# Token-major keys without TensorE: VectorE block transposes and ScalarE copies from unit 8 on, with 112-wide value tiles

## The chip, the cores and the metric

The kernel runs on one core of one Trainium2 chip. The metric is device microseconds of one execution. TensorE (PE) does matmuls and loads weights (PEld), VectorE (DVE) and ScalarE (ACT) do elementwise work, GpSimd (POOL) only sets constants up, and SyncE (SP) issues nearly all DMA transfers; the finished output is sent by ScalarE.

## The reference

The program is a gated linear attention with a complex decay, followed by a gated feed-forward layer without a nonlinearity. There are 4 batches, 8 heads, 768 tokens and a head width of 48; the feed-forward layer goes from 384 (8 x 48) to 1,536 and back for all 3,072 tokens.

```python
mag = np.sqrt(a_re * a_re + a_im * a_im)
scale = np.minimum(mag, 0.999) / (mag + 1e-06)
a_re_n, a_im_n = (a_re * scale, a_im * scale)
for t in range(S):
    new_re = ar * S_re - ai * S_im
    new_im = ar * S_im + ai * S_re
    S_re, S_im = (new_re + k[t] outer v[t], new_im)
    y[:, :, t] = np.einsum('bhd,bhde->bhe', q[:, :, t], S_re)
x = y with the heads side by side, one row per token
return (x @ w_a) * (x @ w_b) @ w_out
```

All arrays are 32-bit floats.

## The kernel before

**Units.** The 3,072 tokens are cut into 12 units of 256: unit u holds chunk u % 6 (128 tokens) of two batches. For each unit there are three stages. Unit 5 and unit 11 are the last chunks of their batch pairs; they hand no state on.

**Preparation, `prep(u)`** (L200), mostly VectorE with some ScalarE. It scales the decays of the unit (`scale`, L167, a chain of ScalarE functions and VectorE products that uses the tile `a_t` of another unit as scratch), forms their running complex products (L227, L233 over 8 tokens, then L262 and L268 over the 16 blocks, then L289 and L294), takes reciprocals (L297 to L320), and multiplies keys and queries by them in the tile `qk` (L324, and L309 in `times_p`). Keys and queries have the feature in the partition and the token in the free dimension: `qk` is [128, 3, 2, 514], three groups of 128 features, real and imaginary part, 256 query tokens and 256 key tokens. The scaling of the next unit's decays is interleaved with the products of this unit, from the fifth step of the loop at L224 on. `prep` ends with the load of the decays of unit u + 2 (L333), into the buffer that `a_t` of this unit leaves (two buffers).

**Stacking, `stack(u)`** (L338): ten SyncE DMA issues copy `qk` into `stk`, where each head has its 96 rows (48 real, 48 imaginary) in partitions 0 to 95.

**Attention, `attn(u)`** (L365), for each batch i of the two and each half of the heads: score matmuls (L379) and their causal masking by VectorE (L382); TensorE transposes of the keys against an identity (L390) and ScalarE copies of them from PSUM into tiles `kt`, token-major, two buffers (L394); output matmuls of values with masked scores and of the old state with the queries (L422), whose sum ScalarE and VectorE split in two parts `xh` and `xl` (L424, L430); and the state update, matmuls of `kt` with the values (L445), added to the state tiles `us` (L452, L456). Units 5 and 11 leave out transposes and states.

Values arrive as tiles of 512 columns, 128 for each pair of heads: head one in columns 0 to 47, head two in 80 to 127, zeros between. The state tiles are laid out alike.

**Feed-forward**: `gemm1` (L483) computes for each of 12 slices f of the hidden layer both products, 18 matmuls into a PSUM tile `ab` (three buffers); ScalarE copies one half out (`h_t`, L497, two buffers), VectorE multiplies it by the other half (L498), and ScalarE and VectorE split the product into `hh` and `hl` (L499, L500). `gemm2` (L503) multiplies these with the output weights two slices later (`LAG`). ScalarE copies the finished output into `o_sb` (L646, three buffers, which also serve the weight conversion at the start) and sends it.

**Order.** The loop over w (L650) runs the feed-forward of unit w and, from slice 6 on (5 for w = 0), the attention of unit w + 1, piece by piece between the slices. After slice 10 (11 in the first three turns) the rest of the preparation of unit w + 2 is written, then its stacking, then the load of keys and queries and the start of the preparation of unit w + 3. A planner then sets the order of each engine's queue from priorities and estimated durations; score masking, output matmuls and the copies of the feed-forward have raised priority (`ATTN_FIRST`, `MOE_FIRST`). Within a queue, instructions run in that order, and a waiting one holds those behind it.

The load of the values of unit w + 1 stands at the start of the turn:

```python
t = vpool.tile([128, 512], F32, name="v_t")
sync.dma_start(out=t, in_=v_d[u, i])
```

Of the kernel before, what the change touches and what calls it, by code (L numbers as in the profile page):

```python
# [19 lines left out]
C = 128  # L20
# [15 lines left out]
A2_MAX = 2.0 ** 60  # L36
ST = 8
# [8 lines left out]
OWN_FROM = 2  # L46
O_BUFS = 3
# [20 lines left out]
def tile_kernel(ctx: ExitStack, tc: tile.TileContext, a_d, qk_d, v_d, w_d, qn_d, kn_d, vn_d, an_d, out_d):  # L68
# [40 lines left out]
    us = [const.tile([128, 512], F32, name=f"u{i}") for i in range(2)]  # L109
# [90 lines left out]
    def prep(u):  # L200
# [23 lines left out]
        for i in range(1, SUB):  # L224
            pr = small.tile([128, 2, 2, NB], F32, name="pr", bufs=1)
            for o, n in parts:
                vec.tensor_tensor(  # L227
                    out=pr[:, :, :, o:o + n],
                    in0=view(zz, W + at_(i) + 2 * o, [[W, 2], [-W, 2], [2, n]]),
                    in1=tok(slice(1, 3), i - 1, o, n).unsqueeze(1).broadcast_to([128, 2, 2, n]),  # L230
                    op=ALU.mult)
            for o, n in parts:
                vec.tensor_tensor(out=tok(slice(1, 3), i, o, n), in0=pr[:, :, 0, o:o + n],  # L233
                                  in1=pr[:, :, 1, o:o + n], op=ALU.add)
            yield 440 + (next(sg, 0) if i > 3 else 0)
        for _ in sg:
            pass
# [11 lines left out]
        vec.tensor_scalar(out=tt[:, 0], in0=tt[:, 2], scalar1=-1.0, scalar2=None, op0=ALU.mult)  # L249
        if c == 0:  # L250
            b_t = small.tile([128, 3, G, NSB], F32, name="b_t")
            vec.memset(b_t[:, 1, :, 0], 1.0)
            vec.memset(b_t[:, 2, :, 0], 0.0)
        else:
            b_t = bnext.pop(u)
# [27 lines left out]
        yield 1600  # L283

# [44 lines left out]
        for k in range(2):  # L329
            times_p(k, 0 if u else 1, 2)  # L330
            yield 1670
# [20 lines left out]
    def load_v(u):  # L352
        for i in range(2):
            t = vpool.tile([128, 512], F32, name="v_t")
            sync.dma_start(out=t, in_=v_d[u, i])
            v_tiles[u, i] = t
# [3 lines left out]
    for g in range(H // 2):  # L360
        for q, pieces in ((3 * g, [(2 * g, 0)]), (3 * g + 1, [(2 * g + 1, 96)]),
                          (3 * g + 2, [(2 * g, 32), (2 * g + 1, 64)])):
            quads[q % 4].append((q // 4, [(h, g * 128 + off) for h, off in pieces]))

    def attn(u, xh, xl):  # L365
# [3 lines left out]
        ams, kts, xps = {}, {}, {}  # L369
# [16 lines left out]
        def transposes(i, hg):  # L386
            qs, ks = cols(i)
            tp = ps_m.tile([128, 512], F32, name="pm")
            for h4 in range(4):
                pe.transpose(out=tp[:, h4 * KS:(h4 + 1) * KS], in_=stk[0:KS, hg * 4 + h4, ks],  # L390
                             identity=ident[0:KS, 0:KS])
            kt = kvp.tile([128, 4, KS], F32, name="kt", bufs=2)
            with tc.high_priority(offset=ATTN_FIRST):
                act.copy(out=kt.rearrange("p h k -> p (h k)"), in_=tp[:, 0:4 * KS])  # L394
            kts[i, hg] = kt
# [41 lines left out]
        def state(i, hg):  # L437
# [4 lines left out]
            for h4 in range(4):  # L442
                h = hg * 4 + h4
                o = (h // 2) * 128 + (h % 2) * (80 if own else 32)
                pe.matmul(out=kp[0:KS, h4 * n:(h4 + 1) * n], lhsT=kts[i, hg][:, h4, :],  # L445
                          rhs=v_t[:, o:o + n], start=True, stop=True)
            uv = view(ut[0:KS], hg * 256, [[128, 2], [80, 2], [1, 48]])
# [19 lines left out]
        for fn, i, g in order:  # L467
            if not (last and fn in (transposes, state)):
# [3 lines left out]
    def pieces(u):  # L472
        return 8 if u % NCH + 1 == NCH else 16
# [9 lines left out]
    def gemm1(f, xh, xl, ps_ab=ps_ab, moe=moe):  # L483
# [9 lines left out]
        h_t = moe.tile([128, TOK], F32, name="h_t")  # L493
# [154 lines left out]

    pgen = None
    for w in range(NU):  # L650
# [18 lines left out]
        for f in range(NF):  # L669
# [8 lines left out]
            pend.append((w, f, *gemm1(f, *x_cur), os_))  # L678
# [89 lines left out]
```

## Time and profile before

| what | value |
|---|---|
| median of 3 runs | 691.08 us (691.05 to 691.49) |
| the profiled execution's own time | 690.18 us |
| its span in the profile | 688.5 us |
| granted TensorE clock, mean | 0.972 |
| TensorE busy | 644.5 us (94%) |
| VectorE busy | 550.1 us (80%) |
| ScalarE busy | 310.1 us (45%) |
| transposes on TensorE (L390) | 160 recorded, 251 ns each as recorded |
| copies of them on ScalarE (L394) | 40 recorded, 482 ns each |

Matmuls overlap in the pipeline, so their recorded lengths exceed the time that each takes of the engine; the chain of waits gives runs of them with the time they took. The first 68 us prepare unit 0 and convert weights; the output matmuls of the first attention start at 69.8 us. Line numbers such as L390 are those of the kernel before.

### The profile page before, as it was taken

What the parts mean: (1) busy time and instruction counts of PE and PEld (TensorE: products, weight loads), DVE (VectorE), ACT (ScalarE), POOL (GpSimd) and SP (SyncE); (2) the same over time, 40 slices, a digit from 0 to 9 for tenths busy, and PEclk for the clock granted to TensorE, in tenths of its full rate; (3) what the DMA queues carried; (4) which work ended last, traced back from release to release, by engine and by line L of the source; (5) the groups of instructions that cost most, each with busy time, mean ns of one, the idle gap of its engine ahead of it and who ended that gap; (6) DMA issues with size and microseconds to landing.
All of it is one profiled execution on the core that took longest, in us unless ns stands there. A gap on an engine that the chain in (4) does not pass through costs nothing.

```text
span 688.5 us, 14290 instructions
## 1 busy us (share of the span) xinstructions
PE 644.5 (94%) x5842; PEld 608.3 (88%) x5842; DVE 550.1 (80%) x1259; ACT 310.1 (45%) x622; POOL 5.6 (1%) x11
## 2 busy tenths in 40 slices
PE   3547999999999999999999999999999999999996
PEld 1214889899999999999999999999999999999996
DVE  6999899998989989999898898999989963233221
ACT  7357664735445346354363553635542332221221
POOL 3000000000000000000000000000000000000000
PEclk9676999999999999999999999999999999999999
DMA  8963301513314225043160440611500500400000
GB/s 321 402 268 95 121 1 44 143 54 87 115 39 139 63 78 145 16 136 104 29 194 2 122 117 3 178 60 62 155 24 18 153 24 18 108 24 2 24 1 28
DMA packets 30232, 63.94 MB, mean 93 GB/s; under 512 B 3664, under 2 KB 7248, under 8 KB 30160
## 3 DMA queue, kind: packets, MB, share of 16 engines
q1 hardware_dynamic: 26704, 58.23, 27.3%
q10 hardware_dynamic: 3456, 4.72, 1.9%
q8 instruction: 48, 0.79, 0.5%
q14 instruction: 24, 0.20, 0.1%
HBM read 39.32 MB, written 4.72 MB: 64 GB/s over the span
## 4 chain that ended last, share of the span: by engine, by line
PE 66%; DVE 25%; ACT 4%; DMA 2%; issue 2%; SPq 0%; DVEq 0%; ACTq 0%
PE ab L489 33%; PE o L507 16%; PE xp L422 5%; PE pm L379 4%; PE pm L445 3%; DVE a_t L289 3%; DVE qk L309 2%; PE pm L390 2%; DVE h_t L498 2%; DVE hl L500 2%; PE pm L147 1%; DVE z L294 1%; DVE pr L227 1%; DVE am L382 1%; DVE pb L262 1%
## 5 line engine op out<-in xcount | busy, mean ns | idle before, releaser
L489 PE MATMUL ab<-xh,w 128*128 128x256 f32 x1728 | 341.6, 286 | 0.0
L489 PEld LDWEIGHTS ab<-xh,w 128*128 128x128 f32 x1728 | 277.2, 189 | 1.7 <-issue 0.8
L489 PE MATMUL ab<-xl,w 128*128 128x256 f32 x864 | 245.5, 284 | 0.0
L489 PEld LDWEIGHTS ab<-xl,w 128*128 128x128 f32 x864 | 163.0, 189 | 0.6 <-issue 0.2
L507 PE MATMUL o<-w,hh 128*128 128x384 f32 x576 | 152.7, 343 | 0.0
L497 ACT COPY h_t<-ab 128x256 f32<-128x256 f32 x144 | 53.4, 371 | 163.4 <-PE ab L489 163.4
L498 DVE TENSOR_TENSOR h_t<-ab,h_t 128x256 f32<-128x256 f32 x144 | 60.4, 420 | 64.6 <-ACT h_t L497 64.3
L507 PEld LDWEIGHTS o<-w,hh 128*128 128x128 f32 x576 | 96.6, 188 | 1.1 <-issue 1.0
L507 PE MATMUL o<-w,hl 128*128 128x384 f32 x288 | 97.2, 338 | 0.0
L499 ACT CAST hh<-h_t 128x256 fp32r<-128x256 f32 x144 | 58.0, 403 | 78.0 <-DVE h_t L498 76.9
L500 DVE TENSOR_TENSOR hl<-h_t,hh 128x256 fp32r<-128x256 f32 x144 | 60.4, 419 | 16.6 <-ACT hh L499 16.4
L379 PE MATMUL pm<-stk 128*128 128x128 f32 x384 | 54.8, 280 | 2.1 <-DMA stk<-qk 2.0
L147 PE MATMUL ab<-o_sb,ident 128*128 128x384 f32 x42 | 28.1, 764 | 29.7 <-DVE o_sb L138 29.7
L379 PEld LDWEIGHTS pm<-stk 128*128 128x128 f32 x384 | 50.2, 194 | 5.7 <-issue 3.6
L507 PEld LDWEIGHTS o<-w,hl 128*128 128x128 f32 x288 | 54.1, 188 | 0.0
L227 DVE TENSOR_TENSOR pr<-z 128x384 f32<-128x384 f32 (+1 forms) x91 | 47.2, 525 | 1.8
L289 DVE TENSOR_TENSOR a_t<-z,b_t 128x768 f32<-128x768 f32 x48 | 44.7, 947 | 0.1
L147 PEld LDWEIGHTS ab<-o_sb,ident 128*128 128x128 f32 x42 | 9.5, 268 | 39.3 <-DVE o_sb L138 30.3
L309 DVE TENSOR_TENSOR qk<-qk,z 128x1536 f32<-128x1536 f32 (+1 forms) x26 | 42.3, 1626 | 0.2
L422 PE MATMUL xp<-am,v_t 128*32 128x128 f32 x768 | 37.7, 281 | 4.3 <-DVE am L382 4.1
L382 DVE TENSOR_TENSOR am<-pm,mask 128x512 f32<-128x512 f32 x48 | 32.7, 685 | 5.2 <-PE pm L379 4.4
L424 ACT CAST xh<-xp 128x384 fp32r<-128x384 f32 x24 | 11.4, 475 | 49.3 <-PE xp L422 49.1
(107 smaller groups left out, 768.7 us busy)
## 6 DMA issues: line engine op xcount, KB each, us to landing
w<-in_dram SPq DMA_DIRECT2D x36, 384.0 KB, 8.0
qk<-in_dram SPq DMA_DIRECT2D x12, 768.0 KB, 4.9
stk<-qk SPq DMA_DIRECT2D x48, 192.0 KB, 3.3
a_t<-in_dram SPq DMA_DIRECT2D x11, 768.0 KB, 4.3
v_t<-in_dram SPq DMA_DIRECT2D x24, 256.0 KB, 2.7
stk<-qk SPq DMA_DIRECT2D x24, 192.8 KB, 3.3
out_dram<-o_sb ACTq DMA_DIRECT2D x24, 192.0 KB, 1.9
stk<-qk SPq DMA_DIRECT2D x16, 128.0 KB, 3.1
```

Source lines behind the costliest of these rows:

```text
L147: pe.matmul(out=lp[:, 0:n], lhsT=ident, rhs=t, start=True, stop=False)
L227: vec.tensor_tensor(out=pr[:, :, :, o:o + n], in0=view(zz, W + at_(i) + 2 * o, [[W, 2], [-W, 2], [2, n]]), in1=tok(slice(1, 3), i - 1, o, ...
L289: vec.tensor_tensor(out=pz[:, s].rearrange("p (j b e) -> p j b e", j=SUB // 2, e=2), in0=zb[:, 1 + s], in1=view(bb, (1 + k - s) * NB, [[0, ...
L309: vec.tensor_tensor(out=qk4[:, :, k, x0:x1], in0=qk4[:, :, 1, x0:x1], in1=z[:, k].rearrange("p (j t) -> p j t", j=NJ).unsqueeze(2).broadca ...
L379: pe.matmul(out=sp[:, h4], lhsT=stk[:, h, ks], rhs=stk[:, h, qs], start=True, stop=True)
L422: run = pe.matmul(out=xp[qd * 32:(qd + 1) * 32, ti], lhsT=l, rhs=rr, start=st, stop=sp_, tile_position=(0, qd * 32), skip_group_check=True ...
L489: pe.matmul(out=ab[:, m * TOK:(m + 1) * TOK], lhsT=r(w_ab(f, part, m * NJ + i)), rhs=r(xt[:, i, :]), start=n == 0, stop=n == 8)
L497: act.copy(out=h_t, in_=ab[:, 0:TOK])
L498: vec.tensor_tensor(out=h_t, in0=ab[:, TOK:2 * TOK], in1=h_t, op=ALU.mult)
L499: act.copy(out=r(hh), in_=h_t)
L500: vec.tensor_tensor(out=r(hl), in0=h_t, in1=hh, op=ALU.subtract)
L507: pe.matmul(out=os_[tt][:, 0:DM], lhsT=r(ht[:, ts]), rhs=r(w_t[f, 2][:, part, :]), start=(f == 0 and n == 0), stop=(f == NF - 1 and n == 2))
```

## The change

For units 8, 9 and 10, the keys are no longer turned by TensorE. Behind the preparation's multiplication of the keys, VectorE transposes 32 x 32 blocks: four instructions of [128, 384] elements, which write into `a_t` (`turn_keys`). Then ScalarE moves the blocks between quarters of the partitions into the tile `kt`: 16 copies of [32, 384] elements (`place_keys`). The queries are multiplied after that. The attention of these units has 12 pieces in place of 16. Units 0 to 7 are turned as before; unit 11 needs no turned keys.

`kt` becomes one tile for a whole unit, [128, 2, 768], with one buffer. In the preparations from unit 8 on, the scaling of the next unit's decays comes behind the first products rather than among them, and mostly behind the chain over blocks.

Value and state tiles become 112 wide per pair of heads, with the second head at 64 to 111: each value tile is loaded by two transfers, one of 64 and one of 48 columns per pair. `h_t` has one buffer, and odd slices borrow one of `o_sb` (from turn 1 on) or of `kt` (in turn 0 up to slice 5).

```diff
+VG = 112
+VW = H // 2 * VG
+KT_FROM = 8
...
-    us = [const.tile([128, 512], F32, name=f"u{i}") for i in range(2)]
+    us = [const.tile([128, VW], F32, name=f"u{i}") for i in range(2)]
...
-            yield 440 + (next(sg, 0) if i > 3 else 0)
-        for _ in sg:
-            pass
+            yield 440 + (next(sg, 0) if i > 3 and u < KT_FROM else 0)
+        if u < KT_FROM:
+            for _ in sg:
+                pass
...
+        if u >= KT_FROM:
+            yield 500 + next(sg, 0)
         if c == 0:
             b_t = small.tile([128, 3, G, NSB], F32, name="b_t")
...
         yield 1600
+        for cost in sg:
+            yield cost
...
-        for k in range(2):
-            times_p(k, 0 if u else 1, 2)
-            yield 1670
+        if u < KT_FROM or c + 1 == NCH:
+            for k in range(2):
+                times_p(k, 0 if u else 1, 2)
+                yield 1670
+        else:
+            for k in range(2):
+                times_p(k, 1, 2)
+            yield 1740
+            yield from turn_keys(u, a_t)
+            place_keys(u, a_t)
+            for k in range(2):
+                times_p(k, 0, 1)
+                yield 870
...
-            t = vpool.tile([128, 512], F32, name="v_t")
-            sync.dma_start(out=t, in_=v_d[u, i])
+            t = vpool.tile([128, VW], F32, name="v_t")
+            for c0, s0, n in ((0, 0, 64), (64, 80, 48)):
+                sync.dma_start(out=t.rearrange("p (g e) -> p g e", g=H // 2)[:, :, c0:c0 + n],
+                               in_=v_d[u, i].rearrange("p (g e) -> p g e", g=H // 2)[:, :, s0:s0 + n])
...
+    def new_kt(u):
+        kt_tiles[u] = kvp.tile([128, 2, H * KS], F32, name="kt", bufs=1)
+
+    def turn_keys(u, t):
+        for s in range(2):
+            for i in range(2):
+                vec.transpose(out=view(t[:], i * NJ * 64 + s, [[G * 64, 4], [64, NJ], [2, 32]]),
+                              in_=view(qk[:], s * RUN + TOK + i * C, [[32, 4], [2 * RUN, NJ], [1, 32]]))
+            yield 900
+
+    def place_keys(u, t):
+        new_kt(u)
+        src = t.rearrange("p s w -> p (s w)").rearrange("p (t g x) -> p t g x", t=4, g=G)
+        dst = kt_tiles[u].rearrange("p i (j b x) -> p (i j) b x", j=NJ, b=4)
+        for tb in range(4):
+            for pb in range(4):
+                act.copy(out=dst[tb * 32:(tb + 1) * 32, :, pb], in_=src[pb * 32:(pb + 1) * 32, tb])
...
+        if not last and u < KT_FROM:
+            new_kt(u)
...
-            kt = kvp.tile([128, 4, KS], F32, name="kt", bufs=2)
             with tc.high_priority(offset=ATTN_FIRST):
-                act.copy(out=kt.rearrange("p h k -> p (h k)"), in_=tp[:, 0:4 * KS])
-            kts[i, hg] = kt
+                act.copy(out=kt_tiles[u][:, i, hg * 4 * KS:(hg + 1) * 4 * KS], in_=tp[:, 0:4 * KS])
...
-            if not (last and fn in (transposes, state)):
+            if not (last and fn is state or fn is transposes and (last or u >= KT_FROM)):
...
-        return 8 if u % NCH + 1 == NCH else 16
+        return 8 if u % NCH + 1 == NCH else 12 if u >= KT_FROM else 16
...
-        h_t = moe.tile([128, TOK], F32, name="h_t")
+        if spare and f % 2:
+            h_t = spare()[:, 0:TOK]
+        else:
+            h_t = moe.tile([128, TOK], F32, name="h_t", bufs=1)
...
+    def spare_h(w, f):
+        if w > 0:
+            return lambda: moe.tile([128, DM], F32, name="o_sb", bufs=O_BUFS)
+        if f <= ATTN_AT[0]:
+            return lambda: kvp.tile([128, 2, H * KS], F32, name="kt", bufs=1)[:, 0]
...
-            pend.append((w, f, *gemm1(f, *x_cur), os_))
+            pend.append((w, f, *gemm1(f, *x_cur, spare=spare_h(w, f)), os_))
```

More of the change, by code (lines that the diff above doesn't have):

```diff
@@ L360, in tile_kernel @@
     for g in range(H // 2):
-        for q, pieces in ((3 * g, [(2 * g, 0)]), (3 * g + 1, [(2 * g + 1, 96)]),
-                          (3 * g + 2, [(2 * g, 32), (2 * g + 1, 64)])):
-            quads[q % 4].append((q // 4, [(h, g * 128 + off) for h, off in pieces]))
+        for q, pieces in ((3 * g, [(2 * g, 0)]), (3 * g + 1, [(2 * g + 1, 80)]),
+                          (3 * g + 2, [(2 * g, 32), (2 * g + 1, 48)])):
+            quads[q % 4].append((q // 4, [(h, g * VG + off) for h, off in pieces]))
+    kt_tiles = {}
+    def new_kt(u):
[13 more added lines that the diff above has]
+                act.copy(out=dst[tb * 32:(tb + 1) * 32, :, pb], in_=src[pb * 32:(pb + 1) * 32, tb])
     def attn(u, xh, xl):
@@ L368, in attn @@
         last = c + 1 == NCH
-        ams, kts, xps = {}, {}, {}
+        ams, xps = {}, {}
+        if not last and u < KT_FROM:
+            new_kt(u)
         def cols(i):
@@ L443, in state @@
                 h = hg * 4 + h4
-                o = (h // 2) * 128 + (h % 2) * (80 if own else 32)
-                pe.matmul(out=kp[0:KS, h4 * n:(h4 + 1) * n], lhsT=kts[i, hg][:, h4, :],
+                o = (h // 2) * VG + (h % 2) * (64 if own else 16)
+                pe.matmul(out=kp[0:KS, h4 * n:(h4 + 1) * n], lhsT=kt_tiles[u][:, i, h * KS:(h + 1) * KS],
                           rhs=v_t[:, o:o + n], start=True, stop=True)
-            uv = view(ut[0:KS], hg * 256, [[128, 2], [80, 2], [1, 48]])
+            uv = view(ut[0:KS], hg * 2 * VG, [[VG, 2], [64, 2], [1, 48]])
             kv = view(kp[0:KS], 0, [[2 * n, 2], [D if own else 3 * D, 2], [1, D]])
@@ L481, in w_ab, with gemm1 @@
         return w_t[f, m][:, part, b * 128:(b + 1) * 128]
-    def gemm1(f, xh, xl, ps_ab=ps_ab, moe=moe):
+    def gemm1(f, xh, xl, ps_ab=ps_ab, moe=moe, spare=None):
         ab = ps_ab.tile([128, 512], F32, name="ab")
```

## The prediction

> **What bounds the kernel now.** I read the page first, then the stretches of one unit each, then what TensorE waited for.
>
> ```profile
> PE 644.5 (94%) x5842; PEld 608.3 (88%) x5842; DVE 550.1 (80%) x1259; ACT 310.1 (45%) x622; POOL 5.6 (1%) x11
> ...
> 419.00:469.00 50.00, 49.87 (x499) 48.70 (x491) 46.10 (x104) 25.43 (x48) 0.00 (x0) 1.00 0.27 83
> 469.00:520.00 51.00, 50.76 (x510) 49.73 (x506) 47.15 (x99) 23.56 (x46) 0.00 (x0) 1.00 0.28 81
> 520.00:570.00 50.00, 50.00 (x505) 49.02 (x500) 40.57 (x94) 15.96 (x35) 0.00 (x0) 1.00 0.24 67
> 570.00:621.00 51.00, 51.00 (x504) 50.13 (x498) 14.94 (x34) 12.79 (x32) 0.00 (x0) 1.00 0.18 50
> ...
> PE pm L390 <- DVE am L382: 0.5, 1, 0.5
> ```
>
> The columns of the stretches are busy time of PE, PEld, DVE, ACT and POOL, then clock, DMA share and GB/s. In the 202 us from 419 to 621, where the attention of units 7 to 10 runs, TensorE is idle 0.4 us in all, at full granted clock; the last row is a wait just ahead of that, 0.5 us in unit 7 for a masked score tile from VectorE. So TensorE bounds this part: a microsecond taken from it is a microsecond off the end, as long as nothing it waits for comes later. VectorE is second: idle 3.9, 3.9 and 9.4 us in the first three stretches, then 36 us. ScalarE is idle for half of each stretch or more.
>
> The change touches units 8, 9 and 10, so I looked there for TensorE's transposes (from the chain of waits in order of time: start, length, what) and for what surrounds them (the timeline).
>
> ```profile
> 470.79 0.56 PE pm L390 x5
> 482.86 0.81 PE pm L390 x8
> 521.63 0.48 PE pm L390 x4
> 533.69 0.66 PE pm L390 x8
> 571.48 0.81 PE pm L390 x8
> 584.01 0.66 PE pm L390 x8
> ...
> 468.24 0.47 PE L390 MATMUL pm<-ident,stk 96*128 96x96 f32 x3
> 467.51 1.28 DVE L382 TENSOR_TENSOR am<-pm,mask 128x512 f32<-128x512 f32 x2
> 519.68 0.43 PE L422 MATMUL xp<-am,v_t 128*32 128x128 f32 x8 [0.24 <-DVE am L382]
> ```
>
> Unit 8 has 16 transposes: four at 468.24 (three recorded), then the output matmuls, which need the masked scores that VectorE ends at 468.79, then the other twelve. Unit 9 is alike: four, a wait of 0.24 us for the masked scores, then twelve. In unit 10 all 16 stand behind them.
>
> **What the change removes from TensorE.** The 12, 12 and 16 transposes that stand on the chain: 0.56 + 0.81, 0.48 + 0.66 and 0.81 + 0.66, together 3.98 us. The first four of units 8 and 9 (4 x 0.66/8 = 0.33 us each) I take at nothing: there TensorE would wait for the masked scores instead. If those come earlier, 0.66 more is gained, the upper end with 4.6 us. The lower end is a gain of 1.47, unit 10's alone, should VectorE's lateness eat the other two.
>
> The row says 0.083 us for one transpose in a run of eight. The Trainium skill, "TensorE: Matmul & The Clock Gate" (Part 4: PE-mode transpose), gives some 390 ns for one alone and 275 ns inside a kernel. By that, an estimate, 48 of them would be 13 us; this trace disagrees, since here each is issued behind the one before.
>
> **What it adds to VectorE.** Per unit four block transposes of 128x384, and the two key and query multiplications of 1,536 elements become four of 768. No row shows a block transpose. The groups nearest to it:
>
> ```profile
> L134 DVE TENSOR_SCALAR o_sb<-w 128x384 uint32<-128x384 uint32 x36 | 12.5, 351 | 1.2 <-ACT w L142 0.6 <-DMA w<-in_dram 0.4
> L227 DVE TENSOR_TENSOR pr<-z 128x384 f32<-128x384 f32 x77 | 42.9, 557 | 1.8
> L309 DVE TENSOR_TENSOR qk<-qk,z 128x1536 f32<-128x1536 f32 x22 | 38.5, 1750 | 0.2
> L309 DVE TENSOR_TENSOR qk<-qk,z 128x768 f32<-128x768 f32 x4 | 3.8, 940 | 0.0
> L142 ACT CAST w<-o_sb 128x384 fp32r<-128x384 f32 x36 | 18.1, 510 | 10.9 <-DVE o_sb L138 10.5
> L394 ACT COPY kt<-pm 128x384 f32<-128x384 f32 x40 | 18.0, 482 | 7.9 <-PE pm L390 7.9
> ```
>
> One transpose lies between 0.351 us (one input, dense) and 0.557 us (two inputs, strided); it has one input but strided runs of 32, so I take 0.45, the middle. A form that runs at half the rate would be about 768 elements' worth, 0.94. Splitting the multiplications adds 2 x (2 x 0.94 - 1.75) = 0.26. Per unit 4 x 0.45 + 0.26 = 2.1 us (1.7 to 2.5; 4.0 at half rate), 6.2 us in all. A saving is excluded, since VectorE loses no instruction. The Trainium skill, "Vector Engine (DVE) Microarchitecture Reference" (3.8), has the transpose sustain one element per cycle per lane; no run here shows it.
>
> What hides it: VectorE works ahead. The timeline of it, of SyncE's queue and of TensorE's first scores of each unit:
>
> ```profile
> 434.86 0.96 DVE L211 TENSOR_TENSOR z<-a_t,sc 128x768 f32<-128x768 f32 x1
> 477.71 1.82 DVE L211 TENSOR_TENSOR z<-a_t,sc 128x768 f32<-128x768 f32 x2
> 521.33 1.83 DVE L211 TENSOR_TENSOR z<-a_t,sc 128x768 f32<-128x768 f32 x2
> ...
> 429.23 0.34 SPq L355 DMA_DIRECT2D v_t<-in_dram  x1
> 431.16 0.33 SPq L158 DMA_DIRECT2D a_t<-in_dram  x1
> 434.89 6.79 SPq L346 DMA_DIRECT2D stk<-qk  x10
> 483.12 7.19 SPq L346 DMA_DIRECT2D stk<-qk  x10
> 533.81 8.19 SPq L346 DMA_DIRECT2D stk<-qk  x10
> ...
> 465.31 1.95 PE L379 MATMUL pm<-stk 128*128 128x128 f32 x16
> 515.92 1.95 PE L379 MATMUL pm<-stk 128*128 128x128 f32 x16
> 566.60 1.95 PE L379 MATMUL pm<-stk 128*128 128x128 f32 x16
> ```
>
> L211 opens the preparation of units 9, 10 and 11, so the ones of 8, 9 and 10 end at 434.9, 477.7 and 521.3. Their rows are stacked from 434.89, 483.12 and 533.81 on, and first read at 465.31, 515.92 and 566.60. Between the end of the stacking's issue and the scores lie 23.6, 25.6 and 24.6 us. Two microseconds per unit go into that, if VectorE's queue puts the masking of the next scores ahead of preparation that has time, as it does now (L382 at 467.51 runs in the midst of unit 9's preparation). Without this cover each would stand on the way to the masked scores: that is the first rival.
>
> **What it adds to ScalarE.** Per unit four copies of 0.482 go and 16 of 32 x 384 come. The nearest row with as many elements per partition is L142, 0.510 us, though on 128 partitions; I take it whole, 8.2 us, net 6.2 per unit. The lower bound is nothing saved per element but the fixed part, for which L394's 0.482 is the nearest. ScalarE has 24.6, 27.4 and 34.0 us idle in the three stretches. In front of a waiting h_t or hh copy, one such copy costs at most 0.5 us; TensorE uses the h_t tiles two gemms later, so this is taken at nothing. Without that cover it would be 0.5 us for each of the copies that meet one.
>
> **What it moves.** The key tile is one buffer now, so the copies of unit 8 wait until unit 7's last state matmul has read it, and those of 9 until unit 8's has; the load of a(u+2) must wait for those copies, as they read a_t, where it waited only for L324. The scaling of the next a is moved behind the chain of b_t.
>
> ```profile
> 440.18 0.64 PE pm L445 x8
> 490.79 0.64 PE pm L445 x8
> ...
> 437.06 1.49 ACT L178 ACTIVATE a_t<-a_t 128x1536 f32<-128x1536 f32 x1
> 450.66 0.95 DVE L193 SCALAR_TENSOR_TENSOR sc<-sc,a_t 128x768 f32<-128x768 f32 x1
> 458.36 0.95 DVE L289 TENSOR_TENSOR a_t<-z,b_t 128x768 f32<-128x768 f32 x1
> a_t<-in_dram SPq DMA_DIRECT2D x11, 768.0 KB, 4.3
> v_t<-in_dram SPq DMA_DIRECT2D x24, 256.0 KB, 2.7
> stk<-qk SPq DMA_DIRECT2D x48, 192.0 KB, 3.3
> ```
>
> Worked out for unit 8: key tile free at 440.8, copies until 440.8 + 8.2 = 449, a(10) issued then instead of at 431.2 and landed 4.3 us later, at 453. Its scaling takes 14.5 us (437.06 to 451.61), so to 468, and unit 9's next step, which overwrites the same scratch, L289, starts there rather than at 458.4: 10 us late. Unit 9's preparation then ends at 477.7 + 10 + 2 = 490, its key tile is free at 490 too (491.4 less the 1.4 saved), the copies end at 498, a(11) lands at 503 and is scaled by 517.5. Unit 10's L289 would have come at 477.7 + 23.5 = 501.2 (as 458.36 lies 23.5 behind 434.86), so that preparation ends 16 + 2 us late, at 539. Its stacking, 8.2 to issue and 3.3 to land, is in by 551, against scores at 566.6 - 2.5 = 564. So the cover shrinks from some 24 us to 13 and is not used up. While VectorE waits for the scaling, it has no backlog in front of the masking, which helps the masked scores if anything.
>
> SyncE: if the load of a(10) stood ahead of unit 8's stacking, this would start at 449 instead of 434.9 and be in by 449 + 0.3 + 6.8 + 3.3 = 460, 5 us before the scores. The queue does not have to follow the source order: the load of v for unit 8 at 429.23 is written behind that stacking in the source and was issued ahead of it.
>
> Edits taken at nothing. v comes in four transfers of 256- and 192-byte rows instead of two of 2,048-byte rows; in the units of the steady part it is issued 20 us or more before use. At the start it shares the queues with the weights; VectorE waited for weights 0.4 us in all (L134's row), so I keep 0, and as the end +0.4, that wait doubled. The Trainium skill, "DMA: Bandwidth & Descriptors" (Specifications), asks for 512 bytes or more per transfer for line rate; by it these rows fall under the line, and the landing time in the next trace will show it. h_t keeps two buffers in effect: odd ones borrow from the output tiles or the key tile. Only in unit 0 from the seventh gemm on is there one, where the next copy may wait for the last reader by under 1 us, behind three PSUM buffers. The 112-wide tiles change no instruction's size.
>
> **Sum.** The profiled execution took 690.18 us with a span of 688.5. Less 3.98 it gives 686.2. The median of the runs shown is 691.08, 0.9 above that execution, so the forecast is 691.08 - 4.0 = 687.1, with its own range of 686.0 to 688.8 (4.6 plus half a microsecond of vanished waits, to a gain of 2.3 when one unit's is lost).
>
> **Rivals.**
> 1. VectorE's additions come through to the masked scores (slower). Place: L382 of units 8 and 9, where the chain had VectorE at work without a break and TensorE waiting 0.24 us. Price: the additions of units 8 and 9, 2 x 2.1 = 4.2 us late at unit 9, against which only the savings behind it count (1.14 + 1.47): +1.6 us, 692.7; at 0.94 per transpose 8.0 - 2.6 = +5.4, 696.5. It decides once the additions before each masking exceed VectorE's idle time, 3.9 us per stretch: 2.1 is under it, 4.0 is not. The Trainium skill's rule in "VectorE: DVE Perf Modes" (Rules for kernel authors), to put 128x128 transposes on TensorE, speaks for this side; no row here has a block transpose to test it.
> 2. The transposes were filler. If masked scores stay where they are in units 8 and 9, TensorE waits in place of transposing; only unit 10's 1.47 is left: 689.6. For it: the 0.24 us wait. Against it: most of the transposes stand behind the masking, with gemms to follow.
> 3. The gain is paid back on SyncE's queue. If ScalarE, busy half of the time, needs 16 us rather than 8.2 for its copies, and the stacking does stand behind the load that waits for them, unit 8's stack is in by 440.8 + 16 + 10.4 = 467.2, 2 us behind its scores, and unit 9's by 490 + 16 + 10.8 = 516.8 against 514.5, 2.3 behind: 4.3 us of new waits against 4.0, 691.4. For it: the copies share a queue with the h_t and hh copies. Against it: the row at 429.23. The same time comes out if the planner, which lays all queues anew because buffers change from unit 0 on, leaves a few new waits before 400 us.
>
> **How the numbers follow.** Forecast 0.60; rival 1 0.17; rival 2 0.12; rival 3 0.11. Less than 0.2%, 1.4 us, cannot be told from no change here. Rival 2 lies half in that band, rival 3 mostly: faster 0.60 + 0.07 + 0.02 = 0.69, same 0.05 + 0.08 = 0.13, slower 0.17 + 0.01 = 0.18. The range leaves out a tenth on each side: from 685.6, where all 48 transposes and the waits of units 8 and 9 go, to 692.7, rival 1 without half-rate transposes.
>
> **What would show it.** Right: no L390 rows after 450; per unit 16 ScalarE copies near 0.5 us and four VectorE transposes near 0.45; TensorE still idle under 1 us from 419 to 621, unit 10's first scores some 2.5 us earlier than 566.6, and the end 4 us earlier. Wrong: TensorE waiting for L382, or for the stacking DMA, by a microsecond or more in units 8 to 10; a transpose above 0.9 us; the first 400 us longer than before.

## The result: slower by 0.6%

The changed kernel takes 695.34 us (median; 695.08 to 695.88), the kernel before, run beside it, 691.07 us. The ratio is 1.0062, 95% interval 1.0045 to 1.008. The forecast was 687.1 us, with a range from 685.6 to 692.7; the measured time lies above it.

From here on L numbers are those of the kernel being shown. In the changed kernel L421 are the score matmuls (L379 before), L424 the masking, L462 the output matmuls, L540 to L543 the copies and products of the feed-forward, L182 to L196 the scaling, L297, L302 and L311 later steps of the preparation, L393 the block transposes, L403 the ScalarE copies.

The same view of the stretches of one unit each as was shown of before, and what TensorE waited for from 419 us on (total, times, longest):

```profile
419.00:469.00 50.00, 48.79 (x457) 47.42 (x445) 41.66 (x101) 30.44 (x61) 0.00 (x0) 1.00 0.29 82
469.00:520.00 51.00, 49.21 (x480) 48.19 (x480) 43.97 (x99) 28.52 (x56) 0.00 (x0) 1.00 0.28 79
520.00:570.00 50.00, 48.96 (x477) 47.73 (x478) 39.77 (x91) 22.82 (x48) 0.00 (x0) 1.00 0.24 66
570.00:621.00 51.00, 48.40 (x461) 47.05 (x460) 27.91 (x55) 13.71 (x30) 0.00 (x0) 0.97 0.19 49
...
PE pm L421 <- DVE am L424: 5.9, 3, 2.6
PE xp L462 <- DVE am L424: 0.4, 2, 0.2
```

TensorE's idle time in these 202 us is 6.6 us, where it was 0.4, and nearly all of it is three waits for a masked score tile, one in each of units 8, 9 and 10. VectorE, which is late here, is not fuller than before: it is idle for 8.3, 7.0 and 10.2 us of the first three stretches, where it was idle for 3.9, 3.9 and 9.4.

The three waits in TensorE's timeline (idle time before the instruction in brackets), then the granted clock behind the third (the number after the five engines):

```profile
469.49 0.71 PE L421 MATMUL pm<-stk 128*128 128x128 f32 x4 [1.50 <-DVE am L424]
520.70 0.71 PE L421 MATMUL pm<-stk 128*128 128x128 f32 x4 [1.78 <-DVE am L424]
573.39 0.94 PE L421 MATMUL pm<-stk 128*128 128x128 f32 x6 [2.60 <-DVE am L424]
...
574.00:576.00 2.00, 2.00 (x47) 1.87 (x50) 2.00 (x5) 0.00 (x0) 0.00 (x0) 0.69 0.03 8
576.00:578.00 2.00, 2.00 (x31) 1.61 (x24) 0.82 (x1) 0.48 (x1) 0.00 (x0) 0.50 0.00 0
```

Behind the wait of 2.60 us the clock falls to 0.69 and 0.50 for 4 us. Counted as time lost, an estimate, that is 2 x 0.31 + 2 x 0.50 = 1.6 us. What waits in the first three rows are scores of the unit's second batch, which now stand in front of the output matmuls, where transposes stood.

What VectorE did in front of the masks of units 9 and 10:

```profile
516.55 0.96 DVE L192 SCALAR_TENSOR_TENSOR a_t<-a_t 128x768 f32<-128x768 f32 x1 [0.67 <-ACT a_t L190]
517.43 0.42 DVE L543 TENSOR_TENSOR hl<-o_sb,hh 128x256 fp32r<-128x256 f32 x1
517.76 0.95 DVE L194 SCALAR_TENSOR_TENSOR sc<-a_t,sc 128x768 f32<-128x768 f32 x1
518.75 0.96 DVE L196 SCALAR_TENSOR_TENSOR sc<-sc,a_t 128x768 f32<-128x768 f32 x1
519.63 0.42 DVE L541 TENSOR_TENSOR h_t<-ab,h_t 128x256 f32<-128x256 f32 x1
519.96 0.68 DVE L424 TENSOR_TENSOR am<-pm,mask 128x512 f32<-128x512 f32 x1
...
571.45 0.95 DVE L297 TENSOR_TENSOR a_t<-z,b_t 128x768 f32<-128x768 f32 x1
572.32 0.42 DVE L543 TENSOR_TENSOR hl<-h_t,hh 128x256 fp32r<-128x256 f32 x1
572.65 1.28 DVE L424 TENSOR_TENSOR am<-pm,mask 128x512 f32<-128x512 f32 x2
```

The last three products of the scaling of unit 11, whose first one waits for ScalarE, run just ahead of unit 9's masks; in unit 10 it is a piece of unit 11's preparation. In unit 8 the same three products, of unit 10's scaling, and then L297 end 0.3 us before the masks start at 468.8. The queue has this order, so the masks wait for work that serves scores 50 us later and more.

The added instructions in the groups by form (busy, mean ns), and the value loads:

```profile
L403 ACT COPY kt<-a_t 32x384 f32<-32x384 f32 x48 | 24.5, 511 | 3.0 <-DVE a_t L393 1.9 <-PE pm L485 0.4
L317 DVE TENSOR_TENSOR qk<-qk,z 128x768 f32<-128x768 f32 x16 | 15.2, 948 | 0.1
L393 DVE STREAM_TRANSPOSE a_t<-qk 128x384 f32<-128x384 f32 x12 | 6.2, 552 | 0.0
...
v_t<-in_dram SPq DMA_DIRECT2D x24, 128.0 KB, 2.7
v_t<-in_dram SPq DMA_DIRECT2D x24, 96.0 KB, 3.0
```

### The profile page after: what moved, and what is told of

It reads as the page before. It is cut to its first block, busy times and chain, and to the rows that moved or that the text cites. A ratio compares the mean times of both kernels' runs of the same rounds, so it can differ in the third digit from the quotient of the medians.

```text
span 693.4 us, 14243 instructions
## 1 busy us (share of the span) xinstructions
PE 643.1 (93%) x5794; PEld 606.2 (87%) x5794; DVE 557.1 (80%) x1277; ACT 328.8 (47%) x658; POOL 5.5 (1%) x11
## 4 chain that ended last, share of the span: by engine, by line
PE 54%; DVE 28%; ACT 8%; DMA 5%; issue 2%; SPq 2%; DVEq 0%; ACTq 0%
PE ab L529 26%; PE o L550 12%; PE xp L462 5%; PE pm L421 4%; ACT kt L403 3%; PE pm L485 3%; DMA w<-in_dram 3%; DVE a_t L297 3%; DVE qk L317 2%; DVE hl L543 2%; DVE pr L230 2%; DVE am L424 2%; DMA stk<-qk 1%; DVE pb L268 1%; PE pm L432 1%
## 5 line engine op out<-in xcount | busy, mean ns | idle before, releaser
L421 PE MATMUL pm<-stk 128*128 128x128 f32 x384 | 56.1, 283 | 7.8 <-DVE am L424 5.9
L421 PEld LDWEIGHTS pm<-stk 128*128 128x128 f32 x384 | 50.4, 195 | 12.9 <-DVE am L424 6.8
L540 ACT COPY h_t<-ab 128x256 f32<-128x256 f32 x75 | 27.7, 369 | 71.5 <-PE ab L529 68.8
L541 DVE TENSOR_TENSOR h_t<-ab,h_t 128x256 f32<-128x256 f32 x75 | 31.4, 419 | 31.3 <-ACT h_t L540 31.1
L540 ACT COPY o_sb<-ab 128x256 f32<-128x256 f32 x66 | 24.4, 369 | 64.2 <-PE ab L529 64.0
L542 ACT CAST hh<-h_t 128x256 fp32r<-128x256 f32 x75 | 30.2, 402 | 45.2 <-DVE h_t L541 44.7
L541 DVE TENSOR_TENSOR o_sb<-ab,o_sb 128x256 f32<-128x256 f32 x66 | 27.7, 420 | 27.2 <-ACT o_sb L540 27.1
L297 DVE TENSOR_TENSOR a_t<-z,b_t 128x768 f32<-128x768 f32 x48 | 44.7, 949 | 0.1
L317 DVE TENSOR_TENSOR qk<-qk,z 128x768 f32<-128x768 f32 (+1 forms) x32 | 43.2, 1350 | 0.2
L542 ACT CAST hh<-o_sb 128x256 fp32r<-128x256 f32 x66 | 26.6, 403 | 34.2 <-DVE o_sb L541 33.1
L462 PE MATMUL xp<-am,v_t 128*32 128x128 f32 x768 | 38.5, 286 | 4.2 <-DVE am L424 4.2
```

The source lines that it names most:

```text
L297: vec.tensor_tensor(out=pz[:, s].rearrange("p (j b e) -> p j b e", j=SUB // 2, e=2), in0=zb[:, 1 + s], in1=view(bb, (1 + k - s) * NB, [[0, ...
L317: vec.tensor_tensor(out=qk4[:, :, k, x0:x1], in0=qk4[:, :, 1, x0:x1], in1=z[:, k].rearrange("p (j t) -> p j t", j=NJ).unsqueeze(2).broadca ...
L421: pe.matmul(out=sp[:, h4], lhsT=stk[:, h, ks], rhs=stk[:, h, qs], start=True, stop=True)
L462: run = pe.matmul(out=xp[qd * 32:(qd + 1) * 32, ti], lhsT=l, rhs=rr, start=st, stop=sp_, tile_position=(0, qd * 32), skip_group_check=True ...
L540: act.copy(out=h_t, in_=ab[:, 0:TOK])
L541: vec.tensor_tensor(out=h_t, in0=ab[:, TOK:2 * TOK], in1=h_t, op=ALU.mult)
```

## The experiments

The letters in the expectations: L, the load of `a_t` held back by the copies makes the scaling late; V, VectorE's own added time; S, ScalarE's added time; F, the transposes on TensorE were filler, and it waits without them; M, the moved scaling alone; O, the other edits (112-wide tiles, loads in two parts, `h_t`). A, later, is V, S and L together.

One table for all. "Stretch" is the time from unit 7's first output matmul to unit 11's, in one profiled execution (418.73 to 620.79 before, 202.06 us); "waits" is TensorE's waits for masked scores from 400 us on, in us, and the longest.

| kernel | ratio to before (95%) | stretch | waits |
|---|---|---|---|
| before | 1 | 202.1 | 0.7 (0.5) |
| changed | 1.0062 (1.0045 to 1.008) | 207.3 | 6.6 (2.6) |
| e1 no turning | 1.0006 (0.9995 to 1.0018) | 202.2 | 0.7 (0.5) |
| e2 scaling moved alone | 1.0013 (1.0004 to 1.0023) | 202.6 | 1.1 |
| e3 no copies | 1.008 (1.0063 to 1.0098) | 203.9 | 4.4 (2.0) |
| e4 copies of a constant | 1.0099 (1.0083 to 1.0116) | 204.7 | 4.0 (1.4) |
| e5 no block transposes | 1.0044 (1.003 to 1.0058) | 206.2 | 4.9 (2.0) |
| e6 block transposes added | 1.0086 (1.0066 to 1.0105) | 208.8 | 4.8 (2.0) |
| e7 products for transposes | 1.0076 (1.0059 to 1.0093) | 208.9 | 6.6 (2.6) |
| e8 some work behind masks | 1.0045 (1.0028 to 1.0061) | 205.1 | 5.7 (3.4) |
| e9 removal alone | 0.9953 (0.9936 to 0.997) | 198.3 | 0.9 (0.5) |
| e10 copies added | 1.014 (1.0123 to 1.0156) | 210.0 | 5.3 (1.8) |
| e11 unit 10 alone | 0.9999 (0.9987 to 1.001) | 201.7 | 0.8 (0.5) |
| e12 more work behind masks | 1.0018 (1.0006 to 1.0031) | 203.3 | 3.8 (3.1) |
| e13 scaling behind masks too | 0.9958 (0.9944 to 0.9972) | 198.6 | 0.7 (0.4) |
| e14 as e13, copies on GpSimd | 1.0046 (1.003 to 1.0061) | 205.7 | 1.2 (0.6) |
| e15 changed, copies on GpSimd | 1.019 (1.0173 to 1.0206) | 214.8 | 7.6 (2.7) |

A single execution lies up to 3 us from its kernel's median (e4's is its lowest), so stretches tell waits apart, and ratios tell times.

**e1, e2: the edits beside the turning.** e1 sets the start of the turning behind the last unit; e2 moves the scaling as the change does, and no more.

```diff
-KT_FROM = 8
+KT_FROM = 12          # e1 and e2
+SG_FROM = 8           # e2: the scaling's place hangs on this one
```

> All edits of the change except the turning: no unit is turned by VectorE, TensorE transposes stay in all units, the scaling keeps its old place; what is left of the change is one key buffer per unit, borrowed h_t buffers, 112-wide tiles and split loads of v. If the loss comes from turning (theories L, V, S, F below), this is the kernel before: 691.1 within 0.2%. Theory O, the other edits: 693 or more.

> As the run without turning, but from unit 8 on the scaling of the next unit's decays stands behind the chain over blocks, as in the change. Loads of a are as early as before. Theory M, the new place of the scaling alone: VectorE reaches the masking of units 8 and 9 late, TensorE waits 1.5 us or more at each, 694 to 695. Theory L, that the late load of a is what makes the scaling late: 691.1 within 0.2%, no wait of TensorE over 0.5 us.

Both stand at the time of before within 0.13%. O and M are out, and the loss comes with the turning of units 8 to 10.

**e3, e4: is it the late load?** e3 leaves out the 16 copies (the states of units 8 to 10 then come from unit 7's keys); e4 lets them read a constant instead of `a_t`, so the copies hold no load back.

```diff
-            place_keys(u, a_t)
+            kt_tiles[u] = kt_tiles[KT_FROM - 1]                               # e3
...
-                act.copy(out=dst[...], in_=src[pb * 32:(pb + 1) * 32, tb])
+                act.copy(out=dst[...], in_=w_t[tb, 0]...[pb * 32:(pb + 1) * 32, 0:G])   # e4
```

> The changed kernel without ScalarE's 16 copies per unit (left out: the turned keys never reach the key tile, and the states of units 8 to 10 read the keys of unit 7). VectorE's transposes stay. Loads of a are then held by nothing but the transposes. Theory V, VectorE's own 2.5 us per unit: still 694 to 695. Theories L and S (the copies, through the load of a or through ScalarE's time): waits of TensorE under 0.5 us, and the 4.0 us of transposes gained, 687 to 688. Theory F, that TensorE's transposes only filled a wait: 690 to 691.

> The changed kernel with ScalarE's 16 copies per unit taken from a constant weight tile instead of the transposed blocks (left out: the turned keys, the states of units 8 to 10 get weights for keys). The copies take the same time and wait for the same key tile, but no longer hold the load of a. Theory L: the waits at units 8 and 9 (1.7 and 2.0 us) go, the one at unit 10 (2.6 us and the slower clock behind it) stays, about 691.5. Theory S, ScalarE's time alone: 695 as in the changed kernel. Both gone: 687 to 688.

Neither is faster than the changed kernel. But the loads are only partly freed, since VectorE's transposes write into `a_t` too. The load for unit 10 goes out at 437.3 us in e3 and 436.7 in e4 (450.3 in the changed kernel, 432.2 in e1), the load for unit 11 at 485.3 and 490.3 (501.7 and 473.8). The masks are late all the same. So neither the copies' own time nor the load that waits for them is needed for it; a part of the delay of the loads is left in both.

**e5, e6, e7: is it VectorE's time?** e5 puts a pause in the written order in place of the four transposes (the keys of units 8 to 10 are then not turned); e6 adds four transposes that nobody reads to e1, and TensorE's own stay; e7 does a product over the same elements in place of each transpose.

```diff
-            yield from turn_keys(u, a_t)
+            yield 1800                              # e5
...
+            if 8 <= u < NU - 1:                     # e6, on e1
+                yield from turn_keys(u, a_t)
...
-                vec.transpose(out=..., in_=keys)
+                vec.tensor_tensor(out=..., in0=keys, in1=keys, op=ALU.mult)   # e7
```

> The changed kernel without VectorE's four block transposes per unit (left out: ScalarE's copies read the scratch as it is, so the states of units 8 to 10 get wrong keys). The copies, the late load of a and the split multiplications stay. Theory V, VectorE's added time: the waits for masked scores fall to 0.5 us or less, 687 to 689. Theory F, with TensorE's transposes gone there is less of its work between scores and masks, and it waits whatever VectorE has added: waits of 1 us or more at units 8 to 10, 692 to 695.

> The kernel without turning, plus four block transposes per unit on VectorE at the end of the preparation of units 8 to 10, whose result nothing reads; TensorE's transposes stay. Theory V: VectorE is 2 us later at each masking than the planned order allows, so TensorE waits as in the changed kernel and gains nothing: 694 to 697. Theory F: the transposes on VectorE are absorbed, 691 within 0.2%.

> The changed kernel with each block transpose replaced by a product of the same 128x384 elements through the same strides, which VectorE does in about the same time (0.55 us; left out: the turning, so the states of units 8 to 10 get wrong keys). Theory V in its form that the planner knows a product's length but takes a block transpose for much shorter: the queue is laid right, waits 0.5 us or less, 687 to 689. Theory V in its plain form, VectorE is too full for 2 us more: as the changed kernel, 694 to 697. Theory F: as the changed kernel too.

e6 loses 0.86% although all TensorE transposes are there; so additions alone can bring the waits, here in front of unit 9's transposes:

```profile
521.49 0.96 DVE L311 TENSOR_TENSOR a_t<-a_t 128x768 f32<-128x768 f32 x1 [1.22 <-ACT a_t L305]
522.70 1.28 DVE L426 TENSOR_TENSOR am<-pm,mask 128x512 f32<-128x512 f32 x2
...
523.43 0.55 PE L434 MATMUL pm<-ident,stk 96*128 96x96 f32 x4 [2.03 <-DVE am L426]
```

e6 is not VectorE's time alone, though: the loads wait for these transposes too and go out at 438.4 and 489.7 us, 6.2 and 15.9 us later than in e1. And e5, without them, loses 0.44%, so they are not needed for the loss. Its 694.87 us is what F expected; e9 below decides against F. e7 is like the changed kernel, so it is nothing special to the transpose.

**e9, e10: the two halves.** e9 is e1 with TensorE's transposes of units 8 to 10 and the copies of their results taken out and nothing added (the states again from unit 7's keys). e10 is e1 with 16 copies per unit added that nobody reads.

```diff
-            if not (last and fn is state or fn is transposes and (last or u >= KT_FROM)):
+            if not (last and fn is state or fn is transposes and (last or u >= 8)):    # e9
...
+                        act.copy(out=src[pb * 32:(pb + 1) * 32, (tb + 1) % 4],
+                                 in_=src[pb * 32:(pb + 1) * 32, tb])                   # e10
```

> e1 (every other edit of the change, no turning) with one thing taken out: the TensorE transposes of units 8 to 10 and the copies of their results, without anything in their place; the state products of units 8 to 10 read the keys of unit 7 that stand in kt, so these values are left out of the computation. Two theories. F: that TensorE's transposes gave the masked scores time to come, and that without them TensorE waits; then the waits for am that the changed kernel has (5.9 us in its second half) stay here, and the time is 692 us or more. A: that what the change adds (VectorE's transposes, ScalarE's copies, the late load) makes the preparation late on VectorE, and the masks stand behind it; then the waits stay near e1's 0.7 us and the time is that of e1, 691.4, less the 4.0 us of the prediction's first term: 687.4, between 686.5 and 689.

> e1 with the TensorE transposes kept, and 16 copies of 32x384 by ScalarE per unit added for units 8 to 10, from one quarter of the scratch tile to another; nobody reads them. So ScalarE's added time stands alone, without VectorE's transposes, without the wait for kt and without split multiplications. F expects e1's time, 691 to 692. If ScalarE's time alone is harmless, as the prediction took it, also 691 to 692. A in its form S: the copies hold ScalarE's part of the next preparation back, VectorE then gets to its products late and the masks stand behind them: 694 to 697, with waits for am of 3 us or more.

e9 settles F: the removal alone is worth 0.47%, and no wait comes of it. The first and the last row of its stretch, and of the kernel before:

```profile
419.08 0.43 PE L464 MATMUL xp<-am,v_t 128*32 128x128 f32 x8
617.34 0.43 PE L464 MATMUL xp<-am,v_t 128*32 128x128 f32 x8
```

```profile
418.73 0.43 PE L422 MATMUL xp<-am,v_t 128*32 128x128 f32 x8
620.79 0.43 PE L422 MATMUL xp<-am,v_t 128*32 128x128 f32 x8
```

198.26 against 202.06 us: 3.80 us less, of which the medians (687.84 and 690.75 us) show 2.9. And e10 shows how copies of 0.5 us on an engine that is half idle cost some 9 us. First e1, then e10: the first ScalarE step L216 of unit 9's preparation, the last key product L332 of that preparation, L216 of unit 10's preparation, a late step of that one on VectorE, and unit 9's mask; in e10 also a wait of VectorE for ScalarE.

```profile
437.21 0.84 ACT L216 ACTIVATE z<-z 128x768 f32<-128x768 f32 x1 [0.20 <-DVE z L214]
472.75 0.96 DVE L332 TENSOR_TENSOR qk<-qk,a_t 128x768 f32<-128x768 f32 x1
480.06 0.85 ACT L216 ACTIVATE z<-z 128x768 f32<-128x768 f32 x1
514.00 0.96 DVE L326 TENSOR_TENSOR a_t<-a_t 128x768 f32<-128x768 f32 x1 [0.42 <-ACT a_t L313]
519.40 0.68 DVE L424 TENSOR_TENSOR am<-pm,mask 128x512 f32<-128x512 f32 x1
```

```profile
441.76 0.43 DVE L546 TENSOR_TENSOR h_t<-ab,h_t 128x256 f32<-128x256 f32 x1 [2.00 <-ACT h_t L545]
442.29 0.85 ACT L216 ACTIVATE z<-z 128x768 f32<-128x768 f32 x1
478.54 0.95 DVE L332 TENSOR_TENSOR qk<-qk,a_t 128x768 f32<-128x768 f32 x1
488.80 0.85 ACT L216 ACTIVATE z<-z 128x768 f32<-128x768 f32 x1
522.27 0.96 DVE L326 TENSOR_TENSOR a_t<-a_t 128x768 f32<-128x768 f32 x1 [0.41 <-ACT a_t L313]
524.47 0.68 DVE L429 TENSOR_TENSOR am<-pm,mask 128x512 f32<-128x512 f32 x1
```

The copies of unit 8 stand in ScalarE's queue in front of L216, which starts 5.1 us later, and in front of the feed-forward's copies, for which VectorE waits. The preparation is one chain between VectorE and ScalarE, so VectorE comes to L332 5.8 us later. The copies of unit 9 follow and add to it: the next L216 is 8.7 us later, and VectorE's L326 8.3. L326 still stands in front of the masks, which come 5.1 us later (unit 8's output matmuls were 1.7 us later already). ScalarE's time does not stand alone here, as the expectation has it: the copies read `a_t`, so the loads go out at 442.3 and 488.8 us, 10.1 and 15.0 us later than in e1. No run delays the load and adds nothing, so the shares of L, V and S stay open.

**e11: unit 10 alone.**

```diff
-KT_FROM = 8
+KT_FROM = 10
```

> The change from unit 10 on alone (KT_FROM=10): 16 transposes of TensorE less, four VectorE transposes and 16 copies once; no load of a stands behind these copies, since unit 12 does not exist. F: waits only around unit 10, 1 to 3 us of wait less 1.3 us of removal: 691 to 693. A: the additions fall in one stretch only, in front of unit 10's and unit 11's masks; a wait of 2 to 3 us there as in the changed kernel, with the lowered clock behind it, less 1.3 us: 691 to 693.5. If one stretch has room for them: 689.8, which would speak against A for a single unit and for the late load as what tips it.

No loss and no gain that can be told (0.9999); the waits for masks stay short. One unit's additions found room here, which speaks against a fixed price per addition. It speaks for the late load as a part of the loss, as no load stands behind these additions, but VectorE also had more idle time there before, 9.4 us in the stretch against 3.9. The 1.3 us of removal that this case was to gain don't show in the median, 690.86 us; in the trace TensorE waits 0.7 us for a copy of the output that it didn't wait for before.

**e8, e12, e13: the order on VectorE's queue.** These are the changed kernel with all its instructions, and links that put later work behind the second mask of a unit. e8: behind the masks of units 8 and 9 the rest of the scaling of units 10 and 11 (from L194 of the changed kernel on), behind those of unit 10 the chain over blocks of unit 11 from its fifth step on. e12: also all of unit 10's and 11's preparation that remains at that point. e13: also unit 11's scaling from its first product on.

```diff
+            for ins in held.pop(u):
+                tc.add_manual_dep(ins, masks[u].name, ..., reason="masks first")
```

> The changed kernel, complete, with one order forced in VectorE's queue for each of units 8 to 10: the rest of the next preparation (from the fourth product of the scaling on; for unit 11 from the fifth step of the chain over blocks on) stands behind the masking of the unit's first score tiles. It takes some 2.7, 2 and 4 us of work from in front of the masks. Whatever made VectorE late, if its place in the queue is what costs (theories V and F alike), the waits go and the transposes are gained: 687 to 688. If TensorE then waits for the stacking or h_t instead, 691 or more.

> The changed kernel with the order on VectorE's queue written out further than in e8: behind the second mask of unit 8 stands the rest of unit 10's scaling as in e8, behind that of unit 9 all of unit 10's preparation from the end of the steps within blocks on and unit 11's scaling, behind that of unit 10 all of unit 11's preparation from the first step on. If the wait is one of order alone (VectorE has time enough for all, only the masks stand behind late preparation), the waits for am fall under 1.5 us, the clock stays, and the time is 687.4 to 689.5. If VectorE or ScalarE have no time for the additions, what is held back comes late for the next unit instead: waits of 3 us or more at the following scores, and 693 to 698.

> e12 with all of unit 11's scaling, from its first product on, also behind the second mask of unit 9. If the order on the queues is the cause, no wait for masks over 1 us is left, the clock stays at 1.00 in the stretches from 420 to 623 us, and the time is e9's 687.8 (removal alone) to 689.5, which is faster than before. If VectorE or ScalarE lack the time, the work held back makes a later wait: 691.5 to 695, with a wait of 2 us or more at units 9 to 11.

e8 (694.84 us) and e12 (692.44 us) both miss the time that was expected if order alone costs. e8 removes unit 8's wait, but not units 9's and 10's. e12 leaves one, of 3.10 us at unit 9, and shows what is in front there:

```profile
517.68 0.42 DVE L563 TENSOR_TENSOR hl<-o_sb,hh 128x256 fp32r<-128x256 f32 x1 [0.61 <-ACT hh L562]
518.43 0.96 DVE L197 TENSOR_TENSOR a_t<-a_t 128x768 f32<-128x768 f32 x1 [0.32 <-ACT a_t L195]
519.64 0.68 DVE L441 TENSOR_TENSOR am<-pm,mask 128x512 f32<-128x512 f32 x1
...
521.77 0.42 PE L482 MATMUL xp<-am,v_t 128*32 128x128 f32 x8 [3.10 <-DVE am L441]
```

VectorE waits there for ScalarE, which is busy with steps of the same scaling, for the feed-forward's `hh` too. With that scaling behind the mask as well (e13) the waits are gone:

```profile
516.64 0.68 DVE L444 TENSOR_TENSOR am<-pm,mask 128x512 f32<-128x512 f32 x1
517.57 0.68 DVE L444 TENSOR_TENSOR am<-pm,mask 128x512 f32<-128x512 f32 x1
518.58 0.96 DVE L190 SCALAR_TENSOR_TENSOR a_t<-a_t 128x768 f32<-128x768 f32 x1
...
470.00:521.00 51.00, 51.00 (x534) 49.82 (x523) 39.20 (x81) 25.43 (x52) 0.00 (x0) 1.00 0.28 80
521.00:572.00 51.00, 50.62 (x496) 49.79 (x495) 41.22 (x89) 26.89 (x54) 0.00 (x0) 1.00 0.24 65
572.00:623.00 51.00, 51.00 (x496) 50.13 (x495) 34.12 (x82) 15.20 (x33) 0.00 (x0) 1.00 0.18 49
```

e13 takes 687.81 us, the same as the removal alone (687.84), and beats both kernels: ratio 0.9958. All the transposes, copies and late loads (at 451.5 and 504.6 us) are in it. VectorE and ScalarE had the time; the changed kernel loses it by order.

**e14, e15: the copies on an idle engine.** GpSimd does the 16 copies, in the order of e13 (e14) and in the changed kernel's own (e15).

```diff
-                act.copy(out=dst[...], in_=src[...])
+                nc.gpsimd.tensor_copy(out=dst[...], in_=src[...])
```

> e13 with the 16 copies of 32x384 per unit by GpSimd in place of ScalarE. If the order is the cause, the same time as e13 within 1 us, since ScalarE's 25 us of copies are off the path then. If ScalarE's time is short, faster than e13 by what its waits were. If GpSimd's copies slow VectorE's instructions (its sums and products longer than 0.95 us for 128x768), slower than e13.

> The changed kernel with its own order and the 16 copies per unit by GpSimd. If the order on the queues is the cause, waits for masks stay, from VectorE's transposes and the late load alone: 693 to 697, as in e3 without copies (ratio 1.008). If ScalarE's copies are what makes the loss, the time of the removal: 687.5 to 689.

Both are slower, so "the same within 1 us" was wrong for e14, and e15's 703.81 us lies above both times expected for it. In e14:

```profile
495.63 11.59 POOL L423 COPY kt<-a_t 32x384 f32<-32x384 f32 x16 [42.66 <-ACT o_sb L563]
...
504.18 0.41 DVE L564 TENSOR_TENSOR o_sb<-ab,o_sb 128x256 f32<-128x256 f32 x1
505.56 0.72 DVE L566 TENSOR_TENSOR hl<-o_sb,hh 128x256 fp32r<-128x256 f32 x1
508.06 0.56 DVE L244 TENSOR_TENSOR pr<-z 128x384 f32<-128x384 f32 x1
...
512.81 1.48 ACT L189 ACTIVATE a_t<-a_t 128x1536 f32<-128x1536 f32 x1 [6.62 <-DMA a_t<-in_dram]
...
PE o L573 <- ACT hh L565: 3.1, 1, 3.1
```

The copies end at 507.2, the load of `a_t` goes out behind them at 507.25, and ScalarE stands for 6.62 us on the first step of the scaling, which waits for that load; behind it in the queue is `hh`, for which TensorE then waits 3.1 us. It is the same fault on another queue. How much of the loss comes from VectorE's slower instructions beside GpSimd (last section) wasn't separated. e15 has waits of both kinds, 7.6 us for masks and 3.0 us for ScalarE's copies of the output.

## Why the prediction was wrong

**What held.** The first term, 3.98 us off TensorE, measured 3.80 in e9's stretch, for all 48 transposes, 0.08 us each. A transpose is recorded as 251 ns long; they overlap, and the run of eight in the prediction shows what one costs. The copies took 0.511 us (taken: 0.510). The split multiplications add 2 x (2 x 0.948 - 1.751) = 0.29 us per unit (0.26). A block transpose took 0.552 us, at the upper end, so VectorE's addition is 4 x 0.552 + 0.29 = 2.5 us per unit, not 2.1. The load chain of unit 8 came out within 2 us: copies to 450.2 (449), scaling to 467.6 (468). A value load of 128 KB lands in 2.7 us, as one of 256 KB did, so half the bytes take the same time, but 20 us ahead of use. The Trainium skill, "DMA: Bandwidth & Descriptors" (Specifications), asks for transfers of 512 bytes or more for line rate. The landing times fit that for rows of 256 and 192 bytes, but a fixed time per load would look the same. Nothing in the value loads or `h_t` showed: e1, which has these edits, is at the time of before. Rival 3 did not happen: the changed kernel's TensorE never waits for the stacking from 400 us on, and it begins the stretch 0.9 us earlier than before. Rival 2 (filler) is refuted by e9. And the time itself, 687.1 us, is that of e13 within 0.7 us: the kernel that was forecast is in effect the change with the masks ahead. By the kernel before beside it (690.83 us), e13 gains 3.0 us, not the 4.0 that was forecast.

**The step that failed** is the sentence at the end of the load chain: "While VectorE waits for the scaling, it has no backlog in front of the masking, which helps the masked scores if anything." It follows the condition "if VectorE's queue puts the masking of the next scores ahead of preparation that has time, as it does now". The lateness was worked out, 10 us for unit 9's preparation, and set against the stacking's cover, where it did no harm. But the queue's order stays when the preparation comes late, so the masks come late with it, and TensorE waits 1.50, 1.78 and 2.60 us. For unit 11's preparation, which stands in front of unit 10's masks and brings the longest wait, no lateness was worked out at all. The row read as proof of priority, the mask at 467.51 in the midst of the preparation, shows no more than that what was planned in front of it was on time.

**Rival 1** named the right instruction, the masks of L382, and the side. It left out unit 10, and its condition was wrong: it was to decide once the additions exceed VectorE's idle time of 3.9 us per stretch. The addition stayed under that, 2.5, VectorE even had more idle time than before, and the loss came. e6 shows that 2.2 us per unit of block transposes (4 x 0.552), with the load that waits for them, are enough on this queue, e10 that none on VectorE are needed, and e13 that all of them cost nothing in another order. The price was also too low: it counted the added microseconds once, without the waits of VectorE for ScalarE inside the late chain, and without the clock.

**The sum** over the stretch: 6.3 us more idle, 1.7 us of lowered clock (summed in steps of 2 us), 3.8 us saved, makes +4.2; measured is 207.27 - 202.06 = +5.2. About 1 us stays unexplained.

**What stays open.** Why the planner leaves the masks behind this work was not tried; e7 says only that another kind of instruction in the same place changes nothing. The additions don't sum: transposes alone lose 0.86%, copies alone 1.4%, both with the removal 0.62%. Each kernel gets queues of its own, which may be why; that was not tested. How much of the lateness comes from the late load, from VectorE's time and from ScalarE's is open too, since every addition that brought waits also held the load.

## What to carry to other kernels

An engine's idle time is no cover when its queue is in a fixed order: ask which instruction stands in front of the one that the bounding engine waits for, and what makes that one late, on any engine. When a change makes off-path work later, bind the on-path instructions ahead of it; here this turned a loss of 0.6% into a gain of 0.4%. To price a change, split it into its removal alone and its additions alone, as e9, e6 and e10 do, and look for what an addition holds back besides, as the load of `a_t` here.

## What the runs showed of the hardware

**The clock after short waits.** From 400 us on, in all the kernels here, each wait for masked scores of 2.5 us or more (six, from 2.51 to 3.35) was followed by output matmuls that took 2.8 to 3.6 us in place of 1.95; of the twelve between 1.5 and 2.2 us, five were, from a wait of 1.56 us on. In each of the seven kernels with one such fall of the clock behind a wait for masks, it adds up to 1.7 us over the stretch, whatever the wait. At about 70 us each kernel waits 2.0 to 2.3 us for its first masked scores, and the clock fell behind it in 16 of the 17; it stayed in e10, which had the longest of these waits. The Trainium skill, "TensorE: Matmul & The Clock Gate" (Part 1), speaks of idle gaps over some 3.4 us, in a window that runs freely. These runs agree in that the length of the gap alone does not decide, but shorter gaps were enough here.

**A copy of 32 partitions** of 384 elements costs ScalarE 0.511 us, no less than one of 128 partitions (0.510 for the cast shown before); on GpSimd the mean in e14 was 0.65 us as recorded, and the slowest 16 of them took 11.59 us.

**GpSimd beside VectorE.** During GpSimd's copies most of VectorE's instructions with two inputs from SBUF became longer, `hl` 0.72 us instead of 0.42; the product that reads PSUM stayed at 0.41 (rows of e14 above). The Trainium skill, "GPSIMD Engine Reference" (1. Specifications), names this contention for two SBUF inputs, and this trace agrees.
